# Rearranging the first microseconds of a fused attention and gMLP kernel: load queue, PSUM tiles and the order of two centred blocks

## The chip, the cores and the metric

The kernel runs on one core of one Trainium2 chip. The metric is device time in microseconds (us) of one execution of the whole program, taken as the median of repeated runs. A core has five engines that run side by side and wait for each other through semaphores: TensorE (PE, matmuls and transposes; its weight loads are listed apart as PEld), VectorE (DVE), ScalarE (ACT), GpSimd (POOL), and SyncE (SP), which here only issues DMAs. Matmuls write to PSUM, a small memory of eight banks; the other engines copy from there to SBUF, the main working memory.

## The reference

The input x has 2048 tokens of 512 features in bfloat16. It is normalised once per token (mean taken off, divided by the standard deviation), and the normalised xn feeds two branches whose outputs are added to x:

```
xn  = layernorm(x)                                  # over the 512 features
A   = attention(xn @ wqkv, 32 heads of 16, each token sees itself and the 255 before it) @ wo
z   = gelu(xn @ w_in)                               # 512 -> 2 * 688
z1, z2 = z[:, :688], layernorm(z[:, 688:])
B   = (z1 * (w_sp @ z2 + b_sp)) @ w_out             # w_sp mixes the 2048 tokens
out = x + A + B
```

## The kernel before

The 2048 tokens are cut into 16 blocks of 128. The program has two stages. In the first (up to about 86 us) every block is normalised and transposed, so that the features lie on the partitions (`xnT`), and TensorE computes z in two halves of 688 columns per block (`z_half`, line 325) and q, k and v in 48 units (`qkv_unit`, line 124). In the second stage attention scores, the token mixing and the output products are interleaved by an order written out by hand (`ORDER`, line 61). The second stage is not touched.

The change is in the opening of the first stage. What happens there, in the order in which each engine has it:

- Loads. `load_x(queue, n0, n1)` (line 176) loads blocks n0 to n1-1 of x into `xt`, 128 KB a block. `load_w(queue, half, c0, c1)` (line 184) loads 128-row chunks c0 to c1-1 of one half of w_in, 172 KB a chunk. SyncE issues x block 0, chunks 0 and 1 of the first half of w_in, chunk 2, x blocks 2 and 3, the second half of w_in in two pieces, x blocks 4 to 7, and all of wqkv. ScalarE issues two more: x block 1, and chunk 3 of the first half (lines 191 and 193). A DMA issued from an engine stands in that engine's own order of instructions.
- Warm-up. TensorE multiplies constants into the tile `heat` (line 206), nine times with 512 columns, before it has any data, and once more between the transposes of block 0 and those of block 1.
- The first two blocks go a quicker way than the rest. ScalarE takes the mean of each with one ACTIVATE that also accumulates (`mean_of`, line 298); VectorE takes that mean off (`center`, line 306; block 0 in two pieces of 256 columns); TensorE transposes the four 128-column chunks into a PSUM tile `tp` (`turn_early`, line 317); ScalarE copies the tile to `xcT` (line 323; block 0 in two pieces). The division by the standard deviation is left to the scale of the gelu (line 339), for which VectorE takes the variance (lines 259, 262, 268) and GpSimd the power (line 271).
- Blocks 2 and 3 are normalised on VectorE (line 289) and also transposed on TensorE; all later blocks are transposed by a DMA that SyncE issues (line 312).
- From then on each block n has: first half of z, statistics and normalising of later blocks on VectorE, statistics of the z2 half of the block before (line 353), second half of z, and from block 3 on three or four units of q, k, v.

VectorE runs its instructions in program order. Its work in the opening is a list without holes written by the program: statistics of blocks 0 to 3, normalising 2, 0, 1 and 3, statistics of 4, 5 and so on. The q, k, v units take a PSUM bank from one of two pools of two banks each, "o" and "f"; a unit of v frees its bank with a copy on VectorE (line 154), a unit of q or k with a copy on ScalarE (lines 137 and 140). The tile `heat` is taken from the pool "o", the tiles `tp` from "f".

The opening in the program's own words:

```python
            if n == 0:
                turn_early(0, early[0][1], 2)
                warm_up(1)
            rsx[n] = rstd(mv0, 1)[:, 0:1]
            if n == 0:
                center(1, *early[1], 1)
                turn_early(1, early[1][1], 1)
```

Of the kernel before, what the change touches and what calls it, by code (L numbers as in the profile page):

```python
# [8 lines left out]
P = 128  # L9
BF = mybir.dt.bfloat16  # L10
# [16 lines left out]
NC = D // P  # L27
# [10 lines left out]
EW = 5 * 256  # L38
WARM = 9
EARLY = 2  # L40
# [35 lines left out]
def kernel(  # L76
# [12 lines left out]
    nc = tc.nc  # L89
# [72 lines left out]
    with ExitStack() as actx:  # L162
# [27 lines left out]
        load_x(nc.sync, 0, 1)  # L190
        load_x(nc.scalar, 1, 2)
        load_w(nc.sync, 0, 0, 2)
        load_w(nc.scalar, 0, 3, 4)
        load_w(nc.sync, 0, 2, 3)
        load_x(nc.sync, 2, 4)
        load_w(nc.sync, 1, 0, 2)
# [6 lines left out]

        def warm_up(k):
            for _ in range(k):
                nc.tensor.matmul(
                    heat[:], lhsT=nc.const_aps.tensor(1.0, [P, P], BF), rhs=idle,
                    start=True, stop=True,
                )

        warm_up(WARM)

        nc.vector.memset(mhalf[:], -0.5)
# [99 lines left out]

        def turn_early(n, xn, pieces):
            tp = psum["f"].tile([P, NC, P], BF, name="tp", tag="f")
            for c in range(NC):
                nc.tensor.transpose(
                    out=tp[:, c, :], in_=xn[:, c * P : (c + 1) * P], identity=ident[:]
                )
            dst = xcT[:, n] if n < EARLY else xnT[:, :, n * P : (n + 1) * P]  # L320
            k = NC // pieces
            for c in range(0, NC, k):
                nc.scalar.copy(out=dst[:, c : c + k, :], in_=tp[:, c : c + k, :])

# [67 lines left out]
        for n in range(NB):  # L392
# [21 lines left out]
            if 3 < n < NB - 1:  # L414
# [3 lines left out]
                ks = ks[1:]  # L418
            z_half(n, 1, inside=(lambda: turn_early(2, xns.pop(2), 1)) if n == 1 else None)
            if n == 1:  # L420
                turn_early(3, xns.pop(3), 1)
            if n % 2 == 1 and n >= 3:
# [484 lines left out]
```

## Time and profile before

| what | value |
|---|---|
| median of 3 runs | 255.84 us (255.52 to 256.28) |
| the profiled execution's own time | 255.11 us |
| its span (first to last instruction in the trace) | 253.4 us |
| TensorE busy | 249.5 us, 98% of the span |
| ScalarE busy | 191.3 us, 75% |
| VectorE busy | 178.8 us, 71% |
| GpSimd busy | 17.0 us, 7% |
| DMA | 26.16 MB, mean 103 GB/s |

The times in the trace count from the start of the span. A row of the timeline gives start, duration, engine, line, operation, the tile written and the tiles read, and how many instructions of the kind are merged into the row; in brackets stands how long the engine had been idle, and whose work ended the wait. SPq and ACTq are the queues on which SyncE and ScalarE issue DMAs: such a row is the issue, not the transfer. A matmul's duration includes its latency, so that matmuls overlap: four of 128 columns that last 0.31 us each can take 0.63 us together. The chain of waits follows the work that ended last back to the first instruction. "To landing" is the time from a DMA's issue to the semaphore that says that all of it has arrived.

### The profile page before, as it was taken

To read this page: it belongs to the slowest core of one execution; us is meant where nothing else is said; L and a number is where in the kernel's file an instruction comes from. 1 tells how busy PE (TensorE), PEld (TensorE's weight loads), DVE (VectorE), ACT (ScalarE), POOL (GpSimd) and SP (SyncE) were. 2 spreads that over 40 slices of the span, in tenths; PEclk is the share of its full clock that TensorE was granted. 3 is DMA by queue.
4 is the path that set the end of the run, shared out by engine and by line. 5 is a ranking of instruction groups with operands and counts; after the bars stand their busy time and mean duration, and the time that the engine had idled before them with its cause. 6 is when DMAs were issued, how large, how long until landed. Compare 5 with 4: busy or idle time off the path is not lost.

```text
span 253.4 us, 9090 instructions
## 1 busy us (share of the span) xinstructions
PE 249.5 (98%) x4036; PEld 136.4 (54%) x4036; DVE 178.8 (71%) x373; ACT 191.3 (75%) x229; POOL 17.0 (7%) x53
## 2 busy tenths in 40 slices
PE   8999999999999999999999999999999999999995
PEld 4655555555555455555564555546455555556553
DVE  4997997974556738829486955349688766858974
ACT  5756646536446989989789898989988989988900
POOL 3320212111011000000000000000000000000000
PEclk9999999999999999999999999999999999999999
DMA  6999540039102107781944725458824517742462
GB/s 221 390 161 196 156 83 2 1 64 146 41 0 74 37 17 102 147 125 36 175 73 101 178 54 121 77 115 125 134 86 82 138 34 118 158 92 71 34 80 85
DMA packets 68026, 26.16 MB, mean 103 GB/s; under 512 B 57056, under 2 KB 67472, under 8 KB 67984
## 3 DMA queue, kind: packets, MB, share of 16 engines
q1 hardware_dynamic: 67408, 25.12, 49.6%
q8 instruction: 32, 0.52, 0.9%
q10 hardware_dynamic: 576, 0.44, 0.5%
q14 instruction: 10, 0.08, 0.1%
HBM read 8.41 MB, written 2.10 MB: 41 GB/s over the span
## 4 chain that ended last, share of the span: by engine, by line
PE 91%; DVE 5%; DMA 2%; SPq 1%; issue 0%; POOL 0%; POOLq 0%
PE gf L490 32%; PE zp L333 11%; PE S L635 11%; PE fo L525 9%; PE S L578 8%; PE pj_o L131 6%; PE fo L532 6%; PE pj_f L131 4%; PE pj_f L149 3%; PE pj_o L149 2%; DMA xt<-in_A_x_dram 2%; DVE stats L259 1%; DVE st L353 1%; DVE xn L289 1%; DVE mvt L262 0%; SPq L186 0%
## 5 line engine op out<-in xcount | busy, mean ns | idle before, releaser
L644 ACT ACTIVATE E<-S 128x1024 bf16<-128x1024 f32 x152 | 141.9, 1017 | 14.5 <-PE S L635 13.6
L490 PE MATMUL gf<-z2n,wspT 128*128 128x344 bf16 x512 | 85.7, 310 | 0.0
L490 PEld LDWEIGHTS <-wspT 128*128 128x128 bf16 x512 | 45.5, 98 | 31.8 <-issue 11.3
L663 DVE TENSOR_TENSOR E<-E,maskFD 128x1024 bf16<-128x1024 bf16 (+2 forms) x48 | 38.2, 810 | 8.3 <-ACT E L644 7.8
L333 PE MATMUL zp<-w_in_sb,xnT 128*128 128x344 bf16 x224 | 36.6, 309 | 0.0
L635 PE MATMUL S<-qpad,kT 32*64 32x512 bf16 (+3 forms) x960 | 31.9, 309 | 0.0
L585 DVE STREAM_TRANSPOSE ot<-S 128x1024 f32<-128x1024 f32 x16 | 20.0, 1247 | 14.5 <-PE S L578 14.4
L333 PEld LDWEIGHTS <-xnT 128*128 128x128 bf16 x224 | 21.8, 98 | 14.0 <-DMA xnT<-xn 0.3
L496 DVE SCALAR_TENSOR_TENSOR u<-gf,b_all,z 128x344 bf16<-128x344 f32 x32 | 18.1, 567 | 12.8 <-PE gf L490 11.4
L525 PE MATMUL fo<-w_out_sb,uT 128*128 128x512 bf16 (+2 forms) x102 | 25.3, 368 | 0.0
L635 PEld LDWEIGHTS <-kT 32*64 32x64 bf16 x960 | 10.8, 102 | 21.6 <-issue 20.6
L578 PE MATMUL S<-E,v_y 64*32 64x256 bf16 (+2 forms) x960 | 21.6, 231 | 0.0
L578 PE MATMUL S<-E,vx 64*32 64x256 bf16 (+1 forms) x960 | 21.6, 232 | 0.0
L339 ACT ACTIVATE z<-zp 128x688 bf16<-128x688 f32 x14 | 10.4, 744 | 13.9 <-PE zp L333 13.8
L578 PEld LDWEIGHTS <-vx 64*32 64x32 bf16 x960 | 18.1, 90 | 4.5 <-issue 4.4
L546 DVE TENSOR_TENSOR xo<-fo,xo 128x512 bf16<-128x512 f32 (+2 forms) x17 | 11.1, 654 | 13.0 <-PE fo L532 13.0
L131 PE MATMUL pj_o<-xnT,wqkv 128*128 128x512 bf16 x76 | 19.5, 379 | 0.1
L131 PEld LDWEIGHTS <-wqkv 128*128 128x128 bf16 x128 | 12.5, 98 | 12.8 <-issue 0.3
L578 PEld LDWEIGHTS <-v_y 64*32 64x32 bf16 x960 | 18.9, 90 | 0.7 <-issue 0.6
L142 DVE TENSOR_SCALAR qpad<-qt,hmask 128x512 bf16<-128x512 bf16 x32 | 9.7, 346 | 10.6 <-ACT qt L140 10.5
L532 PE MATMUL fo<-wo_sb,oT 128*128 128x512 bf16 (+2 forms) x68 | 17.2, 368 | 0.0
L339 ACT ACTIVATE z2n<-zp 128x688 bf16<-128x688 f32 x14 | 10.4, 744 | 8.8 <-PE zp L333 8.8
(70 smaller groups left out, 207.5 us busy)
## 6 DMA issues: line engine op xcount, KB each, us to landing
xo<-in_A_x_dram SPq DMA_DIRECT2D x16, 128.0 KB, 3.3
out_dram<-xo SPq DMA_DIRECT2D x15, 128.0 KB, 2.4
vx<-v_y SPq DMA_DIRECT2D x16, 102.0 KB, 2.8
xt<-in_A_x_dram SPq DMA_DIRECT2D x3, 512.0 KB, 6.1
wqkv<-in_A_wqkv_dram SPq DMA_DIRECT2D x1, 1536.0 KB, 9.6
w_in_sb<-in_B_w_in_dram SPq DMA_DIRECT2D x3, 344.0 KB, 4.8
w_out_sb<-in_B_w_out_dram SPq DMA_DIRECT2D x1, 640.0 KB, 5.7
wo_sb<-in_A_wo_dram SPq DMA_DIRECT2D x1, 512.0 KB, 7.9
```

Of the source, the lines that this page charges most:

```text
L131: nc.tensor.matmul(pt[:], lhsT=wqkv[:, c, w0 : w0 + P], rhs=xnT[:, c, t0 : t0 + 512], start=(c == 0), stop=(c == NC - 1),)
L333: nc.tensor.matmul(zp[:, j, 0:HALF], lhsT=src[:, c, :], rhs=w_in_sb[:, c, f0 : f0 + HALF], start=(c == 0), stop=(c == NC - 1),)
L339: nc.scalar.activation(out=dst.rearrange("p (j f) -> p j f", j=2), in_=zp[:, :, 0:HALF], func=ACT.Gelu_apprx_tanh, scale=rsx[n] if n < EAR ...
L490: nc.tensor.matmul(gf[:, 0:HALF], lhsT=wspT[t][:, c, :], rhs=z2n[:, c, j * HALF : (j + 1) * HALF], start=(c == 0), stop=(c == NB - 1),)
L496: nc.vector.scalar_tensor_tensor(out=u[:, j * HALF : (j + 1) * HALF], in0=gf[:, 0:HALF], scalar=b_all[:, t : t + 1], in1=z1[:, t, j * HALF ...
L525: nc.tensor.matmul(fo[:, 0:w], lhsT=uTs[t][:, ch, :], rhs=w_out_sb[:, ch, c0 : c0 + w], start=(ch == 0), stop=False,)
L532: nc.tensor.matmul(fo[:, 0:w], lhsT=oTs[t // 2][:, c, q0 : q0 + P], rhs=wo_sb[:, c, c0 : c0 + w], start=False, stop=(c == NC - 1),)
L578: nc.tensor.matmul(o[32 * s : 32 * s + 32, h, q0 : q0 + ni * KB], lhsT=v, rhs=Et[part, s, e, c0 : c0 + ni * KB], start=(i == 0), stop=(i = ...
L585: nc.vector.transpose(out=ot[:].rearrange("p h b j -> p (h b j)"), in_=o[:].rearrange("p h c -> p (h c)"))
L635: nc.tensor.matmul(o.rearrange("p (e q) -> p e q", e=2)[:, :, c0 - b0 : c0 - b0 + ni * KB], lhsT=kT[32 * s : 32 * s + 32, 2 * g + h, k0 : ...
L644: nc.scalar.activation(out=Et[:, 2 * i : 2 * i + 2, :, b0 : b0 + w].rearrange("p s e q -> p (s e) q"), in_=S[i][:].rearrange("p s (e q) -> ...
L663: nc.vector.tensor_tensor(out=v, in0=v, in1=mask, op=ALU.mult)
```

## The change

All loads are issued by SyncE, in the order x block 0, x block 1, chunks 0 and 1 of the first half of w_in, chunk 2, chunk 3, x blocks 2 and 3, and then as before. ScalarE issues none. The warm-up is seven products of 512 columns and three of 128, and the one between the blocks is gone. Block 0's four transposes go into two PSUM tiles of two chunks, each copied by one ScalarE instruction as before (`turn_first`). Block 1 is centred and transposed directly behind block 0, ahead of the two small operations for block 0's standard deviation, and its PSUM tile comes from the pool "o". All other blocks are transposed as before.

```diff
-WARM = 9
+WARM = 7
...
         load_x(nc.sync, 0, 1)
-        load_x(nc.scalar, 1, 2)
+        load_x(nc.sync, 1, 2)
         load_w(nc.sync, 0, 0, 2)
-        load_w(nc.scalar, 0, 3, 4)
         load_w(nc.sync, 0, 2, 3)
+        load_w(nc.sync, 0, 3, 4)
         load_x(nc.sync, 2, 4)
...
-        def warm_up(k):
+        def warm_up(k, n=512):
             for _ in range(k):
                 nc.tensor.matmul(
-                    heat[:], lhsT=nc.const_aps.tensor(1.0, [P, P], BF), rhs=idle,
+                    heat[:, 0:n], lhsT=nc.const_aps.tensor(1.0, [P, P], BF), rhs=idle[:, 0:n],
                     start=True, stop=True,
                 )
 
         warm_up(WARM)
+        warm_up(3, P)
...
-        def turn_early(n, xn, pieces):
-            tp = psum["f"].tile([P, NC, P], BF, name="tp", tag="f")
+        def turn_first(xc):
+            k = NC // 2
+            for c0 in range(0, NC, k):
+                tp = psum["f"].tile([P, k, P], BF, name="tp", tag="f")
+                for c in range(k):
+                    nc.tensor.transpose(
+                        out=tp[:, c, :], in_=xc[:, (c0 + c) * P : (c0 + c + 1) * P],
+                        identity=ident[:],
+                    )
+                nc.scalar.copy(out=xcT[:, 0, c0 : c0 + k, :], in_=tp[:])
+
+        def turn_early(n, xn, tag="f"):
+            tp = psum[tag].tile([P, NC, P], BF, name="tp", tag=tag)
...
-            k = NC // pieces
-            for c in range(0, NC, k):
-                nc.scalar.copy(out=dst[:, c : c + k, :], in_=tp[:, c : c + k, :])
+            nc.scalar.copy(out=dst, in_=tp[:])
...
             if n == 0:
-                turn_early(0, early[0][1], 2)
-                warm_up(1)
+                turn_first(early[0][1])
+                center(1, *early[1], 1)
+                turn_early(1, early[1][1], "o")
             rsx[n] = rstd(mv0, 1)[:, 0:1]
-            if n == 0:
-                center(1, *early[1], 1)
-                turn_early(1, early[1][1], 1)
```

More of the change, by code (lines that the diff above doesn't have):

```diff
@@ L418 @@
                 ks = ks[1:]
-            z_half(n, 1, inside=(lambda: turn_early(2, xns.pop(2), 1)) if n == 1 else None)
+            z_half(n, 1, inside=(lambda: turn_early(2, xns.pop(2))) if n == 1 else None)
             if n == 1:
-                turn_early(3, xns.pop(3), 1)
+                turn_early(3, xns.pop(3))
             if n % 2 == 1 and n >= 3:
```

## The prediction

> **What bounds the kernel now.** I read the page's head first, then the chain of waits of the first 24 us, then the timelines of TensorE, VectorE, ScalarE and SyncE there, and last the DMA views.
>
> ```profile
> span 253.4 us, 9090 instructions
> PE 249.5 (98%) x4036; PEld 136.4 (54%) x4036; DVE 178.8 (71%) x373; ACT 191.3 (75%) x229; POOL 17.0 (7%) x53
> ```
>
> TensorE is busy for all but 3.9 us, so a change of the opening is worth what it shifts the moment from which TensorE runs without a hole. The chain of waits says which moment that is (start, duration, what):
>
> ```profile
> 2.23 4.28 DMA xt<-in_A_x_dram
> ...
> 6.53 0.70 DVE stats L259
> ...
> 9.93 0.69 DVE stats L259
> ...
> 19.21 0.61 DVE v_y L154
> 19.83 0.04 issue
> 19.87 1.02 PE pj_o L131 x4
> ```
>
> The chain runs from the load of x blocks 2 and 3 (issued at 2.23, landed at 6.51) through VectorE, busy without a pause to speak of until 19.83, and only then to TensorE, which waits for a bank of the pool "o" that VectorE's copy of v frees. From there on the chain is practically all TensorE. TensorE's own rows:
>
> ```profile
> 0.84 4.00 PE L206 MATMUL heat<-const-bfloat16-1.0 128*128 128x512 bf16 x9 [0.84 <-PEq L891]
> 4.63 0.63 PE L317 MATMUL tp<-ident,xc 128*128 128x128 bf16 x4
> 5.06 0.63 PE L206 MATMUL heat<-const-bfloat16-1.0 128*128 128x512 bf16 x1
> 5.49 0.63 PE L317 MATMUL tp<-ident,xc 128*128 128x128 bf16 x4
> 5.91 0.70 PE L333 MATMUL zp<-w_in_sb,xcT 128*128 128x344 bf16 x3
> 6.16 0.89 PE L333 MATMUL zp<-w_in_sb,xcT 128*128 128x344 bf16 x5
> 10.10 0.39 PE L317 MATMUL tp<-ident,xn 128*128 128x128 bf16 x4
> 18.43 1.33 PE L333 MATMUL zp<-w_in_sb,xnT 128*128 128x344 bf16 x8
> 19.45 0.31 PE L333 MATMUL zp<-w_in_sb,xnT 128*128 128x344 bf16 x1
> ```
>
> The first useful product starts at 5.91. Of the eight that start at 18.43 the last starts at 19.45, so they lie (19.45 - 18.43) / 7 = 0.146 us apart and TensorE is through at 19.60: it then stands 0.27 us, until 19.87. This is what matters most below: **TensorE is already 0.27 us ahead of VectorE there, and a lead added to it is waited away.**
>
> Two speeds are in these rows. A row's time less one latency, over its count less one, is the spacing: the transposes at 4.63 lie (0.63 - 0.31) / 3 = 0.11 us apart, those at 10.10 (0.39 - 0.22) / 3 = 0.06; the heat products (4.00 - 0.63) / 8 = 0.42. So TensorE runs at about half speed at first; the first two products of z are 6.16 - 5.91 = 0.25 apart, and the five from 6.16 on (0.89 - 0.31) / 4 = 0.145, the full speed. The change-over is near 6.1.
>
> **The change part by part.**
>
> *Loads.* Issues, times to landing and the traffic:
>
> ```profile
> 1.25 0.45 ACTq L186 DMA_DIRECT2D w_in_sb<-in_B_w_in_dram  x1
> 1.27 0.92 SPq L186 DMA_DIRECT2D w_in_sb<-in_B_w_in_dram  x2
> 2.23 0.43 SPq L178 DMA_DIRECT2D xt<-in_A_x_dram  x1
> 3.73 0.47 SPq L178 DMA_DIRECT2D xt<-in_A_x_dram  x1
> xt<-in_A_x_dram SPq DMA_DIRECT2D x1, 128.0 KB, 2.6
> xt<-in_A_x_dram ACTq DMA_DIRECT2D x1, 128.0 KB, 2.8
> xt<-in_A_x_dram SPq DMA_DIRECT2D x1, 256.0 KB, 4.3
> xt<-in_A_x_dram SPq DMA_DIRECT2D x1, 512.0 KB, 6.1
> row<-low SPq DMA_DIRECT2D x1, 0.5 KB, 2.0
> 2.00:2.50 0.50, 0.50 (x2) 0.15 (x1) 0.00 (x0) 0.50 (x1) 0.44 (x3) 1.00 0.42 113
> 2.50:3.00 0.50, 0.50 (x3) 0.22 (x2) 0.00 (x0) 0.50 (x1) 0.00 (x0) 1.00 1.11 377
> ```
>
> (The last two rows are stretches of 0.5 us: busy times of five engines, granted clock, DMA share, GB/s. The clock column says 1.00 although the spacing above is the slow one, so I go by spacing.) Block 0 of x lands at about 3.43, sharing the DMA engines with block 1. About 60 KB have moved by 2.5; at 377 GB/s the rest of both (200 KB) takes 0.53 us, of block 0 alone 0.2. Alone on its queue it could land up to 0.3 us sooner. Bounds: 0, and 0.6 if it took the 2.0 us of the smallest transfer of the trace. I take 0.2.
>
> SyncE now issues two DMAs more ahead of blocks 2 and 3, at 0.92 / 2 = 0.46 each, some 0.05 apart: 2.23 becomes 3.2, and blocks 4 to 7 go from 3.73 to about 4.6. If landing kept its 4.3 us behind the issue, blocks 2 and 3 would land at 7.5, 1.0 late, and the chain with them. But the times to landing grow along the queue (2.6, 4.3, 6.1): these loads wait for the bytes ahead of them. Those are the same 944 KB before and after, only on one queue. So the landing stays near 6.5. Ends: 0 and +1.0; I take 0, as the traffic near 380 GB/s from 2.5 on leaves little idle time to fill. The Trainium skill (DMA: Bandwidth & Descriptors, Issuing engines are not separate DMA queues) says that all issuers' transfers run on the same 16 engines and a second issuer only saves issue time; by it this term is also 0, against +1.0 by the constant landing.
>
> *ScalarE without DMAs, two PSUM tiles, no product in between, block 1 sooner.*
>
> ```profile
> 3.03 0.21 ACT L215 ACTIVATE warm<-warm 128x4 f32<-128x4 f32 x1
> 3.46 0.63 ACT L298 ACTIVATE xc<-xt 128x512 bf16<-128x512 bf16 x1 [0.23 <-DMA xt<-in_A_x_dram]
> 4.61 0.19 ACT L298 ACTIVATION_READ_ACCUMULATOR xc<-xt 128x1 f32 x1
> 5.31 0.65 ACT L323 COPY xcT<-tp 128x256 bf16<-128x256 bf16 x2 [0.51 <-PE tp L317]
> 7.45 0.83 ACT L339 ACTIVATE z<-zp,rs 128x688 bf16<-128x688 f32 x1 [0.70 <-PE zp L333]
> 5.13 0.56 POOL L271 TENSOR_TENSOR rs<-ve,mhalf 128x1 f32<-128x1 f32 x1 [2.65 <-DVE ve L268]
> 4.62 0.17 DVE L262 BATCH_NORM_AGGREGATE mvt<-stats 128x2 f32<-128x6 f32 x1
> 4.92 0.35 DVE L306 TENSOR_SCALAR xc<-xt,mean 128x512 bf16<-128x512 bf16 x1
> 6.53 0.69 DVE L259 BATCH_NORM_STATS2 stats<-xt 128x6 f32<-128x512 bf16 x1 [0.26 <-DMA xt<-in_A_x_dram]
> 9.91 0.69 DVE L259 BATCH_NORM_STATS2 stats<-xt 128x6 f32<-128x512 bf16 x1
> ```
>
> ScalarE is free at 3.24 and waits for x until 3.46. Its two issues of 0.45 cost nothing now, covered by that wait; with them gone it is free near 2.35, which is what lets it use an earlier landing. All of block 0's steps then come 0.2 sooner: transposes at 4.43. The nine heat products would end at 4.63 and stand in the way by 0.2; seven and three small ones end at 0.84 + 7 x 0.42 + 3 x 0.11 = 4.1. The copy at 5.31 waited for the fourth transpose; its own two are done 2 x 0.11 sooner: 5.31 - 0.2 - 0.21 = 4.9, ended by 5.3. Block 1's mean is ready at 4.6 instead of 4.8 (its load is now issued at 1.25, and should land by 3.9, when ScalarE comes to it). VectorE reaches block 1 right behind the aggregate, which ends at 4.79 - 0.2 = 4.59, and no longer behind one more operation: from 4.63 to 4.98, where it was 4.92 to 5.27. The transposes of block 1 start 0.1 later, at 5.1, as the product of 0.43 is gone from 5.06, and take 0.42. **First useful product: 5.5 instead of 5.91** (5.7 if x lands no sooner).
>
> The moved centring adds one wait: with block 1 late, the two operations for block 0's standard deviation queue behind it on VectorE, and GpSimd and the first gelu wait for them. That gelu runs at 7.45 and the power is ready at 5.69, so this is hidden up to 1.8 us. The bank from "o" instead of "f" costs nothing: the next user of either comes at 10 us or later.
>
> The 0.4 us lead is worth less: until 6.1 TensorE is at half speed, so it is 0.2 us of work. TensorE would arrive at 19.40, and its wait grows from 0.27 to 0.47.
>
> *VectorE's chain.* It does the same instructions. It was ready 0.26 before blocks 2 and 3 landed (6.53), and reached block 4 at 9.91, when blocks 4 to 7 had landed at 3.73 + 6.1 = 9.83. So a start sooner at 6.5 would be worth at most 0.08 at 9.9; a late one costs in full.
>
> *Sum.* First product -0.4, of which -0.2 of work, all of it waited away at 19.87; VectorE's chain 0 (from -0.08 to +1.0). I take -0.05 against the profiled execution's 255.11, whose span is 253.4 with 1.7 around it. That execution is 0.73 faster than the median of the runs, 255.84, and I cannot see in one trace where the others lose it. If full speed comes later in some, TensorE and not VectorE is the late one at 19.87 there, and up to the 0.2 of work counts. Between 0 and 0.2 I take -0.1: **255.7 us**, likeliest case's own range 255.2 to 256.2. Differences under 0.3%, 0.77 us, are about what a measurement of this kernel can't tell from none.
>
> **The rivals.**
>
> *Full speed comes later: slower.* TensorE had 5.2 us of work (0.84 to 6.1) before it went to full speed, with only transposes between. The change takes 2.25 of ten long heat products away and leaves TensorE idle or transposing from 4.1 to 5.5. If that stretch doesn't count as work, the build-up could begin again at 5.5, and full speed come at worst 5.2 us later, at 10.7. At half speed d us cost d/2; the 0.47 of wait at 19.87 absorbs some: +d/2 - 0.47 for d us beyond 6.1, +1.8 at d = 4.6. It decides (over 0.77) from d = 2.5. Half way between the ends of its deciding range, +1.3: 257.1. For it speaks that the trace holds no gap as long as this one, against it that transposes already filled 0.8 of the 1.4 us from 4.63 to 6.1 and full speed came all the same. The Trainium skill (TensorE: Matmul & The Clock Gate, Parts 1 and 4) names such a rule: speed is decided in free-running windows of about 3.4 us, and transposes don't count as busy. By that, as an estimate, a missed window costs 3.4 / 2 - 0.47 = +1.2. This trace agrees on a slow first stretch, but one run can't show windows.
>
> *Blocks 2 and 3 land late: slower.* The +1.0 above, 256.8; it decides from a landing at 7.3. The growth of the landing times along the queue speaks against it.
>
> *The ordinary runs lose their time in the opening: faster.* If the 0.73 us by which the median lies above the profiled execution is lost there (loads of two queues that mix otherwise than in this trace, or TensorE late), one queue in order of use may take it back, and VectorE's 0.08 with it: 255.84 - 0.8 = 255.0, or 255.4 with half of it. For it: the rest of the program is one long row of TensorE work with little to vary; against it: nothing in this trace shows where the 0.73 is.
>
> *It doesn't do what it says:* x lands no sooner, first product at 5.7; the time is the same, 255.8.
>
> **How the numbers follow.** No net change, with x sooner or not: 0.5. Full speed late: 0.22. Loads late: 0.08. Time of ordinary runs taken back: 0.2. The two slower cases pass 0.3% nearly always, 0.30; of the faster one the end near 255.0 does, 0.12. The runs shown spread by 0.4 us to either side, which lifts some of the unchanged over the bound: 0.07 more to faster, where the sum leans, and 0.03 to slower. Hence 0.19, 0.48 and 0.33. The range runs from the faster rival's end, 255.0, to 257.0, just under the middle of the clock rival, and leaves out about 0.05 below and 0.15 above.
>
> **What would show it.** Right: x block 0 landed by 3.3; ScalarE's first copy to xcT before 5.0; first product between 5.4 and 5.75; spacing 0.146 from 6.1 on; VectorE at blocks 2 and 3 at 6.5 and at block 4 near 9.9; a wait of about 0.45 us at the fourth block's first unit, which starts at 19.8 again. Wrong: products 0.29 apart far beyond 6.1; VectorE waiting at blocks 2 and 3 until 7; or that unit starting before 19.5, which would mean that the wait for VectorE isn't what I take it for.

## The result, and the profile after

| | median | spread | runs |
|---|---|---|---|
| before, beside it | 255.57 us | 255.33 to 256.28 | 7 |
| after | 256.48 us | 256.19 to 256.78 | 7 |

The ratio is 1.0030, its interval 1.0017 to 1.0043: slower, by 0.9 us in the medians, where no change was forecast. The time lies inside the stated range of 255.0 to 257.0, but in the part of it that belonged to the slower rivals. The profiled execution took 256.78 us, 1.67 more than that of before (255.11). Of these 1.67 the medians differ by 0.91; the rest is that this execution is the slowest of its seven (0.30 above their median), while that of before was 0.46 below the median of the seven beside it (three of the seven are the runs of the table before, whose median of 255.84 was on the high side: the later batches of before, 22 to 35 runs each, have medians of 255.26 to 255.35).

The head of the page after:

```profile
span 255.0 us, 9066 instructions
PE 246.3 (97%) x4012; PEld 135.8 (53%) x4036; DVE 178.8 (70%) x373; ACT 191.2 (75%) x229; POOL 16.9 (7%) x53
```

TensorE is busy 3.2 us less, though the change takes only some 0.9 us of warm-up away (2.25 products at 0.42): TensorE now stands idle where it worked before. The chain of waits of the first 24 us (start, duration, what):

```profile
4.68 7.06 DMA xt<-in_A_x_dram
11.77 0.71 DVE stats L260
...
21.07 0.61 DVE v_y L154
21.68 0.04 issue
21.72 1.02 PE pj_o L131 x4
```

It is the same chain to the same meeting point, but it hangs on another load: not on x blocks 2 and 3, but on blocks 4 to 7, issued at 4.68 and landed at 11.74. The fourth block's first unit starts at 21.72, where it was 19.87: 1.85 us later. Timelines of TensorE, VectorE, ScalarE and SyncE after:

```profile
4.10 0.43 PE L320 MATMUL tp<-ident,xc 128*128 128x128 bf16 x4
5.50 2.58 PE L343 MATMUL zp<-w_in_sb,xcT 128*128 128x344 bf16 x16 [0.39 <-DMA w_in_sb<-in_B_w_in_dram]
9.45 0.76 PE L343 MATMUL zp<-w_in_sb,xcT 128*128 128x344 bf16 x4 [1.38 <-DMA w_in_sb<-in_B_w_in_dram]
19.86 1.33 PE L343 MATMUL zp<-w_in_sb,xnT 128*128 128x344 bf16 x8
21.72 1.02 PE L131 MATMUL pj_o<-xnT,wqkv 128*128 128x512 bf16 x4 [0.53 <-DVE v_y L154]
2.93 0.69 DVE L260 BATCH_NORM_STATS2 stats<-xt 128x6 f32<-128x512 bf16 x1 [1.24 <-DMA xt<-in_A_x_dram]
7.64 0.69 DVE L260 BATCH_NORM_STATS2 stats<-xt 128x6 f32<-128x512 bf16 x1 [1.92 <-DMA xt<-in_A_x_dram]
11.77 0.69 DVE L260 BATCH_NORM_STATS2 stats<-xt 128x6 f32<-128x512 bf16 x1 [0.73 <-DMA xt<-in_A_x_dram]
4.46 0.65 ACT L324 COPY xcT<-tp 128x256 bf16<-128x256 bf16 x2 [0.20 <-PE tp L320]
1.73 1.41 SPq L186 DMA_DIRECT2D w_in_sb<-in_B_w_in_dram  x3
3.18 0.43 SPq L178 DMA_DIRECT2D xt<-in_A_x_dram  x1
4.68 0.47 SPq L178 DMA_DIRECT2D xt<-in_A_x_dram  x1
```

What the reader is to see: x block 0 lands at 2.9 instead of 3.4, and the transposes start at 4.10 and take 0.43 where they took 0.63, so TensorE goes to full speed there (the first two start 0.10 apart, the others 0.06). The first useful product starts at 5.50, the forecast moment. From then on everything is late. VectorE waits for blocks 2 and 3 until 7.64 (6.53 before) and for blocks 4 to 7 until 11.77 (before it came to them at 9.93, behind its own work and without a wait). TensorE waits 1.38 us for the second half of w_in at 9.45, a wait that before did not have; it still has 0.53 to wait for VectorE at 21.72, so there VectorE is the later of the two. DMA issues after, with the median us from issue to landing:

```profile
xt<-in_A_x_dram SPq DMA_DIRECT2D x2, 128.0 KB, 2.1
xt<-in_A_x_dram SPq DMA_DIRECT2D x1, 256.0 KB, 4.4
xt<-in_A_x_dram SPq DMA_DIRECT2D x1, 512.0 KB, 7.1
```

The two later loads of x were issued 0.95 us later than before and did not land sooner behind their issue (4.4 against 4.3, 7.1 against 6.1). The traffic says why. Stretches of 1 us, columns as in the prediction (the last is GB/s); first the two of before, then, in a fence of its own, those of after:

```profile
3.00:4.00 1.00, 1.00 (x4) 0.38 (x3) 0.54 (x1) 0.76 (x3) 0.00 (x0) 1.00 0.99 334
4.00:5.00 1.00, 1.00 (x6) 0.44 (x5) 0.91 (x6) 0.80 (x4) 0.00 (x0) 1.00 1.04 362
```

```profile
3.00:4.00 1.00, 1.00 (x6) 0.45 (x4) 0.94 (x3) 1.00 (x3) 0.00 (x0) 1.00 0.94 189
4.00:5.00 1.00, 0.82 (x11) 0.64 (x10) 0.96 (x5) 0.81 (x4) 0.13 (x1) 1.00 1.00 339
```

The bytes ahead of these loads are the same, but between 3 and 4 us, right behind the first packet of w_in at 2.86, they move at 189 GB/s and not at 334. The DMA share of 0.94 shows that the engines were not idle: their packets took longer. What was lost there isn't made up.

The lost traffic is not the whole delay, though. Each load reports its end in sixteen parts, and the trace has the moment of each. For blocks 2 and 3 the eighth part came at 6.25 before and at 6.61 after, the last at 6.51 and at 7.62. For blocks 4 to 7 the eighth came at 9.65 and at 10.12, the last at 9.88 and at 11.74. So of the two delays, 1.11 and 1.86 us, the eighth part had 0.36 and 0.47; the rest is in the parts behind it, and VectorE waits for the last.

### The profile page after: what moved, and what is told of

The parts are those of the page before. It is cut to its first block, busy times and chain, and to the rows that moved or that the text cites. A ratio compares the mean times of both kernels' runs of the same rounds, so it can differ in the third digit from the quotient of the medians.

```text
span 255.0 us, 9066 instructions
## 1 busy us (share of the span) xinstructions
PE 246.3 (97%) x4012; PEld 135.8 (53%) x4036; DVE 178.8 (70%) x373; ACT 191.2 (75%) x229; POOL 16.9 (7%) x53
## 4 chain that ended last, share of the span: by engine, by line
PE 89%; DVE 4%; DMA 3%; SPq 1%; issue 1%; POOL 0%; POOLq 0%
PE gf L498 32%; PE zp L343 11%; PE S L643 10%; PE S L586 8%; PE fo L533 8%; PE pj_o L131 6%; PE fo L540 5%; PE pj_f L131 4%; DMA xt<-in_A_x_dram 3%; PE pj_f L149 3%; PE pj_o L149 2%; DVE st L363 1%; SPq L186 1%; DVE stats L260 1%; DVE xn L290 1%
## 5 line engine op out<-in xcount | busy, mean ns | idle before, releaser
L533 PE MATMUL fo<-w_out_sb,uT 128*128 128x512 bf16 (+2 forms) x90 | 23.3, 366 | 1.0 <-issue 0.6
L586 PE MATMUL S<-E,vx 64*32 64x256 bf16 (+3 forms) x960 | 21.4, 232 | 0.0
L131 PE MATMUL pj_o<-xnT,wqkv 128*128 128x512 bf16 x71 | 18.9, 379 | 0.7 <-DVE v_y L154 0.5
L540 PE MATMUL fo<-wo_sb,oT 128*128 128x512 bf16 (+2 forms) x64 | 16.3, 366 | 0.6 <-issue 0.6
```

The costliest lines, as they stand in the source:

```text
L131: nc.tensor.matmul(pt[:], lhsT=wqkv[:, c, w0 : w0 + P], rhs=xnT[:, c, t0 : t0 + 512], start=(c == 0), stop=(c == NC - 1),)
L533: nc.tensor.matmul(fo[:, 0:w], lhsT=uTs[t][:, ch, :], rhs=w_out_sb[:, ch, c0 : c0 + w], start=(ch == 0), stop=False,)
L540: nc.tensor.matmul(fo[:, 0:w], lhsT=oTs[t // 2][:, c, q0 : q0 + P], rhs=wo_sb[:, c, c0 : c0 + w], start=False, stop=(c == NC - 1),)
L586: nc.tensor.matmul(o[32 * s : 32 * s + 32, h, q0 : q0 + ni * KB], lhsT=v, rhs=Et[part, s, e, c0 : c0 + ni * KB], start=(i == 0), stop=(i = ...
```

## The experiments

Each kernel is compared with runs of the kernel before on the same chip; "DVE at" are the moments at which VectorE starts on blocks 2 and 3 and on blocks 4 to 7, "3 to 4" is the traffic in GB/s of that microsecond. These last two columns come from the one execution of each kernel that was profiled, the times from all of its executions.

| kernel | median us | before us | ratio (95%) | 3 to 4 | DVE at |
|---|---|---|---|---|---|
| e1_loads_only | 256.43 | 255.27 | 1.0049 (1.0034 to 1.0064) | 174 | 7.13, 10.97 |
| e2_rest_only | 255.45 | 255.27 | 1.0007 (0.9990 to 1.0025) | 340 | 6.91, 10.26 |
| e3_w_in_one | 256.17 | 255.27 | 1.0044 (1.0024 to 1.0065) | 118 | 7.51, 10.87 |
| e4_x1_on_act | 255.56 | 255.34 | 1.0012 (0.9997 to 1.0027) | 325 | 6.60, 9.97 |
| e5_w3_on_act | 256.32 | 255.34 | 1.0040 (1.0020 to 1.0060) | 296 | 7.57, 11.06 |
| e6_one_queue_mixed | 257.04 | 255.34 | 1.0065 (1.0047 to 1.0083) | 312 | 7.83, 11.14 |
| e7_alternating | 255.93 | 255.34 | 1.0017 (0.9992 to 1.0042) | 350 | 6.95, 10.25 |
| e8_touch_w_in | 256.93 | 255.35 | 1.0075 (1.0057 to 1.0092) | 211 | 7.37, 10.69 |
| e9_x01_in_one | 256.14 | 255.35 | 1.0030 (1.0020 to 1.0041) | 316 | 6.73, 10.26 |
| e10_k_first | 255.18 | 255.35 | 1.0000 (0.9987 to 1.0013) | 259 | 6.62, 9.98 |
| e11_rest_k_first | 255.28 | 255.35 | 0.9995 (0.9976 to 1.0013) | 305 | 7.06, 10.42 |
| e12_before_x01_in_one | 255.79 | 255.26 | 1.0018 (1.0006 to 1.0029) | 296 | 6.59, 10.72 |
| e13_short_warm_up | 255.27 | 255.26 | 1.0008 (0.9992 to 1.0024) | 295 | 6.81, 10.18 |
| e14_long_warm_up_k_first | 254.74 | 255.26 | 0.9981 (0.9969 to 0.9993) | 243 | 7.08, 10.44 |
| e15_long_warm_up | 255.30 | 255.26 | 1.0009 (1.0000 to 1.0019) | 326 | 6.58, 10.56 |

**Which part of the change costs?** The changed kernel once more, the loads alone, and all but the loads.

e0_after_again (the kernel after once more, one execution):

> The changed kernel unchanged, for a second trace. If the late landing belongs to the kernel: blocks 4 to 7 land after 10.8 again and TensorE waits for w_in again in the first halves of z, at a span of 254.5 to 255. If it belongs to the one execution that was profiled: they land near 9.9.

It took 256.94 us. Traffic from 3 to 4 us was 161 GB/s, VectorE started on the two loads at 8.52 and 11.88, and TensorE waited 1.80 us for w_in's second half at 9.49: the late landing is no accident of one execution. The last part of the load of blocks 2 and 3 came 0.96 behind the fifteenth (7.53, 8.49), that of blocks 4 to 7 1.06 behind (10.79, 11.85).

e1_loads_only, against the kernel before:

```diff
-        load_x(nc.scalar, 1, 2)
+        load_x(nc.sync, 1, 2)
         load_w(nc.sync, 0, 0, 2)
-        load_w(nc.scalar, 0, 3, 4)
         load_w(nc.sync, 0, 2, 3)
+        load_w(nc.sync, 0, 3, 4)
```

> The kernel before with the load part of the change alone: all loads on SyncE's queue in the new order, none on ScalarE; warm-up, PSUM tiles and order of the blocks as before. Theory L (the loss comes from the loads, which land later from one queue): the whole loss, +0.9 us (0.5 to 1.3) against before, VectorE reaches the statistics of block 4 after 10.8 instead of 9.9, and TensorE waits for w_in. Theory W (the loss comes from the shorter warm-up and the new order of the blocks): within 0.3 us of before.

e2_rest_only is the changed kernel with the reverse of this diff:

> The changed kernel with the loads of before (x block 1 and chunk 3 of w_in on ScalarE's queue): shorter warm-up, two PSUM tiles, block 1 straight behind block 0. Theory L: -0.1 us (-0.4 to +0.2) against before: the first product of z comes near 5.6 instead of 5.91, blocks 2 and 3 land at 6.5 and 4 to 7 at 9.8 as before, and the lead is waited away at the first unit of the fourth block, near 19.8. Theory W: +0.9 us.

The loads alone give 1.0049, the rest alone 1.0007 (the whole change was 1.0030; its interval and that of the loads alone overlap). **The loss is in the loads.** Whether the rest costs or gains a little isn't resolved: its interval runs from -0.3 to +0.6 us. Traffic and VectorE with the loads alone:

```profile
3.00:4.00 1.00, 1.00 (x4) 0.39 (x3) 0.94 (x3) 1.00 (x3) 0.00 (x0) 1.00 0.82 174
7.13 0.69 DVE L259 BATCH_NORM_STATS2 stats<-xt 128x6 f32<-128x512 bf16 x1 [1.33 <-DMA xt<-in_A_x_dram]
10.97 0.70 DVE L259 BATCH_NORM_STATS2 stats<-xt 128x6 f32<-128x512 bf16 x1 [0.45 <-DMA xt<-in_A_x_dram]
```

The same dip (174 GB/s) and the same two late landings, without any of the other edits; here the parts of a load end closer together (blocks 4 to 7: eighth at 10.50, last at 10.95). TensorE in the kernel with all but the loads:

```profile
5.49 4.63 PE L343 MATMUL zp<-w_in_sb,xcT 128*128 128x344 bf16 x28
18.29 1.33 PE L343 MATMUL zp<-w_in_sb,xnT 128*128 128x344 bf16 x8
20.22 1.02 PE L131 MATMUL pj_o<-xnT,wqkv 128*128 128x512 bf16 x4 [0.60 <-DVE v_y L154]
```

The first product starts 0.42 us sooner than before, but at the products ahead of the fourth block's first unit the lead is 0.14 (18.29 against 18.43). The wait there must be read by one measure: the brackets count from the modelled end of the last product (0.60 here, about 0.11 before), the prediction's 0.27 counts from the moment at which TensorE could start the next one, and so counted it is 20.22 - 18.29 - 8 x 0.146 = 0.76 here. Of the 0.49 more, 0.14 is the lead and 0.35 is VectorE, which is later than before in this execution (blocks 2 and 3 from 6.91 on). So what is left of the lead is waited away, as the prediction had it, and the time is the same within the interval.

**Is it the number of issues ahead of blocks 2 and 3?** If the late landing came only from their later issue, fewer issues would cure it. e3_w_in_one, against the kernel after, makes one DMA of the first half of w_in, so that blocks 2 and 3 are issued at 2.20, sooner even than before (2.23):

```diff
-        load_w(nc.sync, 0, 0, 2)
-        load_w(nc.sync, 0, 2, 3)
-        load_w(nc.sync, 0, 3, 4)
+        load_w(nc.sync, 0, 0, 4)
```

> The changed kernel with the first half of w_in as one DMA of four chunks instead of three DMAs: the same bytes in the same order on the same single queue, but x blocks 2 and 3 are issued at 2.25 instead of 3.18, and blocks 4 to 7 near 3.75 instead of 4.68. Theory I (the loads are late because their issue is late, one issue behind the other on SyncE): blocks 2 and 3 land by 6.7 and 4 to 7 by 10.0, and the time is within 0.3 us of before, though the first product waits for all of w_in's first half, until about 5.9. Theory Q (one queue moves less per us than two): they land as late as in the changed kernel (7.6 and 11.7) and it stays +0.6 to +1.0.

```profile
3.00:4.00 1.00, 1.00 (x6) 0.45 (x4) 0.94 (x3) 1.00 (x3) 0.00 (x0) 1.00 0.87 118
7.51 0.69 DVE L258 BATCH_NORM_STATS2 stats<-xt 128x6 f32<-128x512 bf16 x1 [1.74 <-DMA xt<-in_A_x_dram]
6.77 4.24 PE L341 MATMUL zp<-w_in_sb,xcT 128*128 128x344 bf16 x28 [1.40 <-DMA w_in_sb<-in_B_w_in_dram]
```

No. Issued 0.98 us sooner than in the kernel after, blocks 2 and 3 still land at 7.5; the dip is deeper (118), and the first product waits 1.40 us for w_in. So the later issue of blocks 2 and 3 isn't the cause; the slow stretch goes with the late landing. (This edit also joins three DMAs into one; what that does by itself isn't taken apart.)

**Which load has to be on the second queue?** e4_x1_on_act puts x block 1 alone back on ScalarE, e5_w3_on_act chunk 3 of w_in alone (both against the kernel after):

```diff
-        load_x(nc.sync, 1, 2)
+        load_x(nc.scalar, 1, 2)
```

```diff
-        load_w(nc.sync, 0, 3, 4)
+        load_w(nc.scalar, 0, 3, 4)
```

> The changed kernel with x block 1 alone back on ScalarE's queue; chunk 3 of w_in stays on SyncE's. The traffic between 3 and 4 us, 334 GB/s before and 189 in the changed kernel, is what tells. Theory Q (the second queue itself keeps the DMA engines busy while the first packets of w_in are slow): some other packets are there until 3.1, so 250 GB/s or more, blocks 2 and 3 land by 7.0, time between before and the changed kernel, +0.2 to +0.6. Theory M (what counts is which tensors are read at the same time, not from which queue): x block 1 is through before w_in starts either way, near 190 GB/s, +0.9.

> The changed kernel with chunk 3 of w_in alone on ScalarE's queue, where it is issued first, at 0.8; x block 1 stays on SyncE's. Theory Q: 300 GB/s or more between 3 and 4 us, blocks 2 and 3 land by 6.7 and 4 to 7 by 10.0, time within 0.3 us of before; block 0 of x, which now shares the DMA engines with w_in, lands near 3.3 instead of 2.9. Theory M agrees here, since w_in and x are mixed from the start.

SyncE's issue of w_in, the traffic and VectorE with block 1 on ScalarE:

```profile
1.27 1.42 SPq L186 DMA_DIRECT2D w_in_sb<-in_B_w_in_dram  x3
3.00:4.00 1.00, 1.00 (x6) 0.44 (x4) 0.44 (x1) 0.44 (x1) 0.00 (x0) 1.00 1.01 325
6.60 0.69 DVE L260 BATCH_NORM_STATS2 stats<-xt 128x6 f32<-128x512 bf16 x1 [0.25 <-DMA xt<-in_A_x_dram]
```

and with chunk 3 on ScalarE:

```profile
1.75 0.94 SPq L186 DMA_DIRECT2D w_in_sb<-in_B_w_in_dram  x2
4.00:5.00 1.00, 0.08 (x2) 0.00 (x0) 0.94 (x3) 1.00 (x3) 0.00 (x0) 1.00 0.79 179
7.57 0.69 DVE L260 BATCH_NORM_STATS2 stats<-xt 128x6 f32<-128x512 bf16 x1 [0.81 <-DMA xt<-in_A_x_dram]
```

Block 1 alone brings the landing (6.60) and nearly the whole time back (1.0012, not told apart from before). Chunk 3 alone does not (1.0040), though two queues work: the dip only moves by a microsecond, to 4 to 5. "A second queue is enough" falls. (Chunk 3 now also goes out first of all, at 0.81, and x block 0 lands at 3.94, so this run changes more than the queue.) What the good one has in common with before is that chunks 0 and 1 are issued at 1.27 and not near 1.74, while x is still under way.

**Two other orders.** e6_one_queue_mixed has one queue, but the order x0, chunks 0 and 1, x1, chunk 2, chunk 3; e7_alternating has x0, x1 and chunk 2 on SyncE, chunks 0 and 1 and chunk 3 on ScalarE. Against the kernel after:

```diff
-        load_x(nc.sync, 1, 2)
         load_w(nc.sync, 0, 0, 2)
+        load_x(nc.sync, 1, 2)
```

```diff
-        load_w(nc.sync, 0, 0, 2)
+        load_w(nc.scalar, 0, 0, 2)
         load_w(nc.sync, 0, 2, 3)
-        load_w(nc.sync, 0, 3, 4)
+        load_w(nc.scalar, 0, 3, 4)
```

> The changed kernel, all loads still on SyncE's queue, with chunks 0 and 1 of w_in issued ahead of x block 1, so that x follows on w_in's slow first packets. Theory Q: one queue hands each DMA engine its packets in order, so x block 1 waits behind w_in: traffic from 3 to 4 us stays under 230 GB/s, blocks 4 to 7 land after 10.8, +0.8 to +1.3. Theory M: 300 GB/s, and the time is back within 0.3 us of before.

> The changed kernel with the same loads on two queues otherwise than before: x blocks 0 and 1 and chunk 2 on SyncE's, chunks 0 and 1 and then 3 of w_in on ScalarE's. Theory Q: 300 GB/s or more from 3 to 4 us, blocks 2 and 3 land by 6.7, 4 to 7 by 10.0, within 0.3 us of before, the first product as early as in the changed kernel or earlier. Theory M: as Q, since x and w_in are mixed.

The alternating one has no dip (350 GB/s), and VectorE starts on the two loads at 6.95 and 10.25; it is unclear against before (1.0017, 0.9992 to 1.0042), but its median is 0.6 us above, where at most 0.3 was expected: five of its ten executions took 255.21 to 255.50 and five 256.36 to 256.95. The profiled one is the fastest, so its trace can't say what the others lose. The mixed one has the highest median of all:

```profile
7.83 0.69 DVE L260 BATCH_NORM_STATS2 stats<-xt 128x6 f32<-128x512 bf16 x1 [0.82 <-DMA xt<-in_A_x_dram]
6.40 5.86 PE L343 MATMUL zp<-w_in_sb,xcT 128*128 128x344 bf16 x28
```

Here chunks 0 and 1 are issued at 1.27 and the landing is late all the same, with a dip of 204 GB/s between 5 and 6 (it was expected from 3 to 4). So the moment of issue alone isn't the rule either. The second row shows another loss: 28 products take 5.86 us, where at full speed they take 4.24 (the row of e3 above), so for some 3 us TensorE was at half speed: the first twelve products start 0.29 us apart, those from 9.76 on 0.15. In this execution the fourth block's first unit starts without a wait for VectorE, so TensorE, and not the landing, sets its time.

**Is w_in slow because nothing has read it yet?** e8_touch_w_in adds to the kernel after, on ScalarE's queue ahead of all others, a small read of every eighth row of w_in into a scrap tile that nobody uses:

```diff
+        touch = pa.tile([16, 4, 16], BF, name="touch")
+        nc.scalar.dma_start(
+            out=touch[:], in_=B_w_in.rearrange("(c p r) f -> p c r f", p=16, r=8)[:, :, 0, 0:16]
+        )
```

> The changed kernel with one small DMA added, issued from ScalarE at the very start: it reads 32 bytes of every eighth row of w_in into a scrap tile that nobody uses. Theory T (w_in's first packets are slow, 0.3 to 1.3 us instead of 0.06, because nobody has read there before, and on one queue nothing else fills that time): with the rows read ahead the dip between 3 and 4 us goes (300 GB/s or more against 189), blocks 2 and 3 land by 6.8 and 4 to 7 by 10.2, within 0.3 us of before. Theory S (the dip comes from the start of w_in's stream, whatever was read before): as the changed kernel, near 190 GB/s, +0.9 us.

```profile
3.00:4.00 1.00, 1.00 (x6) 0.44 (x4) 0.89 (x2) 0.72 (x2) 0.00 (x0) 1.00 0.85 211
7.37 0.69 DVE L264 BATCH_NORM_STATS2 stats<-xt 128x6 f32<-128x512 bf16 x1 [1.05 <-DMA xt<-in_A_x_dram]
```

The dip stays, and the time is 1.0075 (what the added DMA itself costs is not taken apart). Touching every eighth row does not help; nothing here speaks for that theory.

**One queue without the gap.** x blocks 0 and 1 are 128 KB each. At about 380 GB/s that is 0.34 us, less than the 0.46 us between two issues of SyncE. e9_x01_in_one (against after) and e12_before_x01_in_one (against before) load both with one DMA, so that one queue issues chunk 0 at 1.33, and w_in begins while x still flows:

```diff
-        load_x(nc.sync, 0, 1)
-        load_x(nc.sync, 1, 2)
+        load_x(nc.sync, 0, 2)
```

```diff
-        load_x(nc.sync, 0, 1)
-        load_x(nc.scalar, 1, 2)
+        load_x(nc.sync, 0, 2)
         load_w(nc.sync, 0, 0, 2)
-        load_w(nc.scalar, 0, 3, 4)
         load_w(nc.sync, 0, 2, 3)
+        load_w(nc.sync, 0, 3, 4)
```

> The changed kernel with x blocks 0 and 1 as one DMA on SyncE's queue, so that w_in's first chunks are issued at 1.27, as early as when x block 1 was back on ScalarE's queue, but on one queue. If the early issue of w_in, while x still moves, is what that run gained: no dip from 3 to 4 us (300 GB/s or more), blocks 2 and 3 land by 6.7, 4 to 7 by 10.1, time within 0.3 us of before. If it is the second queue: near 190 GB/s, +0.7 to +1.0.

> The kernel before with all loads on SyncE's queue and x blocks 0 and 1 as one DMA; warm-up and order of before. In the same loads with the short warm-up the traffic from 3 to 4 us was back (316 GB/s) and yet the time was +0.8, with the first 28 products of z at half speed for long (6.29 us instead of 4.3). Theory E (the loads lose by the late issue of w_in alone; the rest of that +0.8 was the late full speed): blocks 2 and 3 land by 6.8, and with the long warm-up the time is -0.2 to +0.3 against before. Theory Q (one queue loses in any case): +0.6 to +1.0 again.

e9, traffic, VectorE and TensorE:

```profile
3.00:4.00 1.00, 1.00 (x6) 0.44 (x4) 0.36 (x1) 0.36 (x1) 0.00 (x0) 1.00 1.02 316
6.73 0.69 DVE L259 BATCH_NORM_STATS2 stats<-xt 128x6 f32<-128x512 bf16 x1 [0.30 <-DMA xt<-in_A_x_dram]
5.82 6.29 PE L342 MATMUL zp<-w_in_sb,xcT 128*128 128x344 bf16 x28
```

e12, VectorE:

```profile
6.59 0.70 DVE L258 BATCH_NORM_STATS2 stats<-xt 128x6 f32<-128x512 bf16 x1 [0.23 <-DMA xt<-in_A_x_dram]
10.72 0.69 DVE L258 BATCH_NORM_STATS2 stats<-xt 128x6 f32<-128x512 bf16 x1 [0.74 <-DMA xt<-in_A_x_dram]
```

With one queue for all, the dip is gone (316 and 296 GB/s) and blocks 2 and 3 land about where they did before. So **one queue does not make the dip by itself**. e12 is 1.0018 where the same loads with two DMAs for x (e1) were 1.0049: about six tenths of the loss come back. About 0.5 us stays, between the two expectations (-0.2 to +0.3, and +0.6 to +1.0), so whether one queue has a part in it is open. In the profiled execution blocks 4 to 7 land at 10.7, but not because they are issued later: in e9 they are issued at the same 4.31 and land at 10.24, and in e12 the eighth of the sixteen parts came at 9.63, as early as before, and only the last at 10.70. That also happens with the loads of before (e15: eighth at 9.68, last at 10.53). e9's median is 0.8 us above before, where at most 0.3 was expected; its profiled execution shows another reason: its 28 products take 6.29 us, late full speed as in e6. It is the slowest of seven (256.65), and how many of the others had this isn't known.

**Does the warm-up's end matter by itself?** e13_short_warm_up takes the change's warm-up alone into the kernel before (seven long products and three short ones, none between the blocks):

```diff
-WARM = 9
+WARM = 7
...
+        warm_up(3, P)
...
-                warm_up(1)
```

> The kernel before with the shorter warm-up alone: seven products of 512 columns and three of 128, none between the blocks. Theory C (the short warm-up makes full speed come one window later in some executions): the times spread to 256.5 and more, in a late one the 28 first products of z last 6 us instead of 4.3, and the median is +0.2 to +0.8. If the warm-up doesn't matter: within 0.15 us of before, with its spread.

1.0008, no difference in the median, where the theory wanted +0.2 or more; one of its twelve executions took 257.06, the others 254.95 to 255.85. The kernel before has such executions too (one of 257.11 in 26). As the cause of the whole 0.9 us it is out.

**Can the lead be kept?** TensorE waits for VectorE's copy of v because the first units that it does are units of v. e10_k_first (against before) and e11_rest_k_first (against e2) do four units of k first, whose banks ScalarE frees:

```diff
-    qkv_list = qkv_list[10:12] + qkv_list[:10] + qkv_list[12:]
+    first = [(0, i) for i in (1, 3, 5, 7)]
+    qkv_list = first + [u for u in qkv_list if u not in first]
```

> The kernel before with one change elsewhere: the four units of k of the first 512 tokens come first, ahead of the two units of v, so that the banks which the fourth block's first unit needs are freed by ScalarE's copy and not by VectorE's. If VectorE's chain holds TensorE at 19.87 and nowhere else: the wait of 0.27 there goes, -0.2 to -0.3 us. If VectorE's chain is met again at the next unit of v: 0.

> The shorter warm-up, two PSUM tiles and block 1 behind block 0, with the loads of before, and the four units of k first. If the lead of TensorE was waited away at the fourth block's first unit (0.6 us there in the run without this order): the lead of 0.2 to 0.4 stays and the wait goes, -0.4 to -0.6 us against before, and this is faster than both kernels. If VectorE's chain is met again at the next unit of v: -0.1 to +0.1.

e10 gives 1.0000 (0.9987 to 1.0013): the wait of 0.27 us before is 0.1% of the time, too little to be seen. e11 gives 0.9995 and not the -0.4 to -0.6 us expected, with two groups of executions, five from 254.55 to 254.81 and three from 256.36 to 256.67, and four in between. The profiled one is of the slower group:

```profile
5.92 5.91 PE L344 MATMUL zp<-w_in_sb,xcT 128*128 128x344 bf16 x28
```

5.91 against 4.24 at full speed: 1.67 us lost, which is about the distance of the two groups. To take this spread away, e15_long_warm_up gives e2 a longer warm-up (eight long products, and a product of 256 columns between the blocks), and e14_long_warm_up_k_first has the same and the units of k first; they differ in nothing else.

```diff
-WARM = 7
+WARM = 8
...
                 turn_first(early[0][1])
+                warm_up(1, 256)
                 center(1, *early[1], 1)
```

> Two PSUM tiles, block 1 behind block 0, the loads of before and the four units of k first, with a longer warm-up that ends where the first transposes can start: eight products of 512 columns and three of 128, and one of 256 between the two blocks' transposes. The same with the short warm-up had five of twelve times at 254.6 and three at 256.4 to 256.7. Theory C: the late ones go, median 254.6 to 254.9, -0.4 to -0.7 against before and faster than both. If the spread has nothing to do with the warm-up: median near 255.2 and the same spread.

> As the run before it, without the four units of k first. Theory C with VectorE's chain holding TensorE near 19.8: -0.1 to -0.2 against before, the lead waited away; without that hold: as the run with k first, -0.4 to -0.7.

TensorE at the fourth block, first with v first (e15), then with k first (e14):

```profile
18.61 1.33 PE L343 MATMUL zp<-w_in_sb,xnT 128*128 128x344 bf16 x8
20.51 1.02 PE L131 MATMUL pj_o<-xnT,wqkv 128*128 128x512 bf16 x4 [0.57 <-DVE v_y L154]
```

```profile
18.47 1.33 PE L344 MATMUL zp<-w_in_sb,xnT 128*128 128x344 bf16 x8
19.63 1.03 PE L131 MATMUL pj_o<-xnT,wqkv 128*128 128x512 bf16 x4
```

With v first TensorE waits there (0.57 in the bracket), with k first it does not. The medians are 255.30 and 254.74: **taking this wait away is worth 0.56 us.** That the two figures are nearly the same may be chance. The profiled execution of e15 took 255.86, more than its median; in it TensorE comes to this point later than before (18.61 against 18.43), and the wait is long because blocks 4 to 7 landed late. The traces don't show the lead itself at work: e14's first product starts at 5.91 and its row at 18.47, both as before, and there it gains the wait of before. e14, with the loads of before, is faster than both kernels (0.9981, 0.9969 to 0.9993), and its twelve executions lie between 254.34 and 255.52.

**What the packets show.** From the trace's records of single packets: of those that start between 2.7 and 4.2 us, how many took over 0.24 us (the typical one takes 0.06), and the longest. Beside it the moment at which VectorE starts on blocks 2 and 3.

```
kernel    over 0.24 us   longest us   VectorE at
loads as before
before         4            0.35         6.53
e13            4            0.67         6.81
e2             6            0.41         6.91
e11            7            0.55         7.06
e15            8            0.47         6.58
e10           14            0.58         6.62
e14           17            0.76         7.08
x blocks 0 and 1 as two DMAs on SyncE, all of w_in behind them there
e1            15            0.81         7.13
e8            16            0.58         7.37
after         18            1.30         7.64
e0            19            0.65         8.52
e3            21            0.95         7.51
other orders
e4             9            0.49         6.60
e5             5            0.68         7.57
e6             9            0.48         7.83
e7             4            0.48         6.95
e9             6            0.63         6.73
e12            9            0.74         6.59
```

The slow packets of this stretch are nearly all packets of w_in. With the loads of before they vary from run to run, from 4 to 17; with the changed loads they are always many (15 to 21), and VectorE's starts don't overlap: 6.53 to 7.08 against 7.13 to 8.52, and for blocks 4 to 7 9.93 to 10.56 against 10.69 to 11.88. In the kernel after, w_in begins no later than before (its first packet starts at 2.86, before at 2.87), and packets of x blocks 0 and 1 go on beside it nearly as long (until 3.11, before until 3.21). Fewer of them start behind w_in's first packet, 32 of 256 against 58. A reading that fits e1, e3, e4, e7, e9 and e12 is that the first packets of w_in are slow when they have the engines to themselves, and that other transfers hide it where they overlap: with the changed loads 21 to 37 packets of x start behind w_in's first, in e4, e7, e9 and e12 51 to 216. This is argued from the timing, not shown, and e13, e14, e5 and e6 speak against it. e13 has few (25) and yet only 4 slow packets; e14 has 53 and yet 17 of them; in e5, where w_in starts ahead of x, the dip comes after w_in's first chunk; e6 has 174 and lands late all the same. **Why those packets are slow, why the last parts of a load can come so late, and the 0.5 us that e12 still loses, stay open.**

## Why the prediction was wrong

**The loads: the step that failed.** The prediction wrote: "these loads wait for the bytes ahead of them. Those are the same 944 KB before and after, only on one queue. So the landing stays near 6.5. Ends: 0 and +1.0; I take 0, as the traffic near 380 GB/s from 2.5 on leaves little idle time to fill." Measured: landing at 7.6, +1.1, just beyond the upper end; VectorE waited at blocks 2 and 3 until 7.64, past the 7 that the prediction had named as a sign of being wrong. The bytes were the same and their speed was not (189 against 334 GB/s from 3 to 4 us). The term was sized by bytes over a rate, and the rate, 377, was read where x flowed, in the half microsecond before w_in's first packet (2.87). The next row of the same view, before and then after:

```profile
3.00:3.50 0.50, 0.50 (x3) 0.22 (x2) 0.04 (x1) 0.26 (x3) 0.00 (x0) 1.00 0.97 292
```

```profile
3.00:3.50 0.50, 0.50 (x3) 0.23 (x2) 0.50 (x1) 0.50 (x2) 0.00 (x0) 1.00 0.92 116
```

So the dip behind w_in's first packet is there before too, only weaker, and "near 380 GB/s from 2.5 on" passed over it. A busy row of traffic showed that there was no idle time to win; it did not show that there was none to lose. A sum of bytes also says when most of a load is there, and the engine waits for its last part: the eighth of sixteen came 0.36 later, the last 1.11. That the loads are the place is shown (e1 against e2, and e4); why the packets slow down is not.

**Blocks 4 to 7 and w_in's second half: not priced.** The bound of +1.0 was made for blocks 2 and 3 and meant to hold the chain. In fact the load behind them was late by 1.85 us at VectorE and took over the chain, and TensorE got a wait of 1.38 for w_in, which VectorE's lateness covered. "A late one costs in full" held: VectorE starts on block 4 1.84 later, and the unit at 21.72 comes 1.85 later. The rival "Blocks 2 and 3 land late", at 0.08 and 256.8, was the one that happened. The growth of the times to landing along the queue, which was held against it, was no argument: times that grow along a queue also grow if the queue slows down.

The Trainium skill (DMA: Bandwidth & Descriptors, Issuing engines are not separate DMA queues) says that a second issuer only saves the sequencer's time to start a DMA, usually small beside the DMA. In the prediction that rule stood for a term of 0. Here the two aren't far apart (0.46 us an issue, about 0.34 us for 128 KB), and two loads moved to the other queue's issuer cost 1.0049. e12 agrees with the rule in that one queue doesn't bring the dip by itself. In e3 the issue time is saved and the landing is late all the same, so what was lost here is not the issue time that the rule speaks of.

**x block 0 sooner: right, larger than taken.** 0.5 us, taken 0.2, bounds 0 to 0.6. In e4, with block 1 on the other queue, it lands at about 3.5 again, so it was the sharing that delayed it.

**First useful product at 5.5: right in time, by another way.** TensorE was ready at 5.11 and waited 0.39 for w_in. The forecast named no such wait; that the two errors met at 5.50 is luck.

**Two PSUM tiles, no product in between, block 1 sooner: right.** Worth nothing that can be seen in the time (e2, 1.0007), because what is left of the lead is waited away at the fourth block's first unit. The forecast was a lead of 0.2 there and a wait of 0.47; e2's trace has 0.14 and, by the same measure, 0.76, as VectorE was 0.35 later too. In e2 the lead went elsewhere than forecast: TensorE was at full speed from the first product on, and two longer steps between products (0.25 at 5.93, 0.43 at 8.37) took most of it.

**The rival "Full speed comes later":** not in the two profiled executions of the kernel after: the spacing is that of full speed from 4.2 on in the one and from 5.1 on in e0. But the prediction's fear wasn't empty: in the profiled executions of e6, e9 and e11 it happened, and cost TensorE 1.6 to 2.0 us (the forecast was half of the delay, up to 2.3, less the wait of 0.47).

**The rival "The ordinary runs lose their time in the opening":** the new order of the loads took nothing back. It fell; and the 0.73 us that it was to explain was in large part the sample of three runs.

## What to carry to other kernels

Moving a load to another queue with the same bytes ahead of it isn't free: look in the trace at the first microsecond of a new stream, price what happens if it slows down there, and do so for every load behind it and not only for the next. Where the first transfers are as short as the interval between two issues, load them with one DMA, or from two engines, so that the next stream starts beside them; here that took back most of the loss (e12, e4). Read when the last part of a load arrives, as the engine waits for that. A lead won at the start is worth only what the next meeting point lets through; move that wait first (here the order of v and k units was worth 0.56 us, e14 against e15).

## What the runs showed of the hardware that was not expected

- With x blocks 0 and 1 as two DMAs on SyncE's queue and all of w_in behind them there, the same bytes moved at 118 to 211 GB/s from 3 to 4 us (after, e0, e1, e3, e8); with the loads of before at 243 to 340 in seven kernels. Single packets of 1376 bytes took up to 1.30 us, the typical one 0.06.
- The sixteen parts of one load can end far apart. With blocks 4 to 7 half were there at 10.12 and the last at 11.74 (after), 9.63 and 10.70 (e12), but 9.65 and 9.88 before.
- TensorE's change to full speed varied from 4.2 us (after) to between 9.3 and 9.9 (e11, e6, e9), where the starts of the products go from 0.29 to 0.15 us apart. The 28 products lost 1.67 us in e11 and 2.05 in e9 against 4.24; the two groups of e11's executions lie 1.6 to 2.1 us apart. The granted clock's column read 1.00 through all of it (e9, 2 to 10 us); only the spacing of the products shows it.
